# Splitting the loads of keys and values by partitions over two DMA queues

## The chip, the cores and the metric

The kernel runs on one core of one Trainium2 chip. The metric is device time in microseconds (us) from the start to the end of one execution; lower is better. The core has engines with instruction streams of their own: TensorE (PE; weight loads are listed as PEld), VectorE (DVE), ScalarE (ACT), GpSimd (POOL) and SyncE (SP). They meet only through semaphores. DMA engines, sixteen of them in the profile, carry data between the chip's memory (HBM) and the on-chip memory (SBUF), which has 128 partitions (rows). A DMA is issued by an engine into that engine's queue.

## What is computed

One decoding step of grouped-query attention over a long cache, in parallel with a small MLP, both added to the input:

```python
Hq, Hkv, Sk, Dh = 32, 8, 65536, 128          # D = 512, Dff = 1792, one token
xn = layernorm(x)
q = (xn @ wq).reshape(1, 1, Hq, Dh)          # 4 query heads share one key head
scores = einsum("bhqd,bhkd->bhqk", q, k) * Dh ** -0.5
o = einsum("bhqk,bhkd->bhqd", softmax(scores), v)
out = x + o.reshape(1, 1, Hq * Dh) @ wo + maximum(xn @ w1, 0) @ w2
```

All is float32. Keys and values are 8 heads x 65536 x 128 x 4 bytes each, 537 MB together, out of the 561 MB that the profile shows as read.

## The kernel before

The attention goes over 8 key heads (`HKV`) with 4 steps (`NP`) each, 32 steps (`STEPS`). A step handles 16384 keys. Its keys are one load of 128 rows (the head dimension) x 16384 float32 into the buffer `ks`; its values are one load of 128 rows x 16384 float32 into `vs`. In both, a row is 65,536 bytes without a break. There is one `ks` and one `vs`, no second buffer of either.

The order of the work is written out by hand, with one instruction stream per engine and semaphores between them:

- **SyncE** issues all of the loads. The first keys are issued near the beginning (line 175), behind the loads of `wq`. Then, head by head, `head(h)` calls `v_load` and `k_load` in turn, so its queue holds keys 0, values 0, keys 1, values 1 and so on. `k_load` (lines 303 to 305) waits for `k_free`, `v_load` (lines 307 to 310) for `v_free`. A `Fori` loop runs seven heads, with the next head's first keys at the end of each; the eighth head follows it. After that SyncE issues `w1` and `w2` into `ks`, and, when `vs` is free, `wo` into `vs`.
- **TensorE** runs a loop of 32 steps. It waits for the keys (`k_in`, line 346), makes the scores from `ks` into PSUM (line 352), takes part in a maximum over partitions (lines 357 to 359), waits for the values (`v_in`, line 363) and for the weights of the softmax (`s_w`), and makes the products with `vs` (line 368).
- **VectorE** transposes the scores (line 384), finds the running maximum, and adds the products into `acc` (lines 408 and 410). Its wait for the last scores frees the keys (`k_free`), its wait for the products frees the values (`v_free`). At the end of a head it reduces (lines 416 to 423).
- **ScalarE** runs 8 x 4 times: wait for `s_bias` (line 428), four exponentials with their sums (line 430), from the second step on one for the rescaling (line 436). At the end of each head it waits for `s_diff` (line 440) and runs one more exponential (line 441).

The lines that matter most:

```python
def k_load(h, n):
    sy.wait_ge(k_free, 1).then_inc(k_free, -1)
    sy.dma_start(ks, k[h, 0, :, n * NT * KEYS : (n + 1) * NT * KEYS]).then_inc(k_in, 16)
...
te.wait_ge(k_in, 16).then_inc(k_in, -16)
...
te.wait_ge(v_in, 16).then_inc(v_in, -16)
```

A DMA adds 16 to its semaphore when it has landed, so 16 means one whole load.

Of the kernel before, what the change touches and what calls it, by code (L numbers as in the profile page):

```python
# [10 lines left out]
ALU = mybir.AluOpType  # L11
AX = mybir.AxisListType
PSUM = bass.MemoryType.PSUM
ENG = mybir.EngineType

P = 128
D = 512
HQ, HKV, DH = 32, 8, 128
# [5 lines left out]
SUB = TW // 32  # L24
KEYS = CT * TW
# [3 lines left out]
NT = 8  # L29
NP = TPC // NT  # L30
# [39 lines left out]
def attention_and_mlp_kernel(  # L70
# [28 lines left out]
    nc = tc.nc  # L99
    scale = float(DH) ** -0.5  # L100
    te, ve, se, ge, sy = nc.tensor, nc.vector, nc.scalar, nc.gpsimd, nc.sync

    def place(name, *shape, rows=P):
        return nc.alloc_sbuf_tensor(name, [rows, *shape], F32).ap()

    def bank(name, *shape):
        return nc.alloc_psum_tensor(name, [P, *shape], F32).ap()

    ks = place("ks", NT * KEYS)
    vs = place("vs", NT * KEYS)  # L110
# [32 lines left out]
    pa, pb = bank("pa", 2, TW), bank("pb", 2, TW)  # L143
    acc_o, acc_z, acc_y, pm = (bank(n, 512) for n in ("acc_o", "acc_z", "acc_y", "pm"))

    names = "k_in v_in tiles scores m_out bias_out a_out w_out o_out k_free v_free q_in d_out f_out f_free"
    (
        k_in, v_in, s_tiles, s_dve, s_max, s_bias, s_alpha, s_w, s_o,
        k_free, v_free, q_in, s_diff, f_out, f_free,
    ) = (nc.alloc_semaphore(n) for n in names.split())  # L150
    PE, DV, AC, GP = (Flow(nc, e, n) for e, n in ((te, "pe"), (ve, "dve"), (se, "act"), (ge, "pool")))

# [32 lines left out]
    def memset(flow, ap, value):  # L185
        return flow.op(lambda e: e.memset(ap, value))

    d = memset(DV, ones, 1.0)
    d = memset(DV, x4, 0.0)
    x4_free = DV.mark  # L190
    d = memset(DV, qcur, 0.0)
# [108 lines left out]
    AC.need(DV.mark)  # L300


    def k_load(h, n):
        sy.wait_ge(k_free, 1).then_inc(k_free, -1)
        sy.dma_start(ks, k[h, 0, :, n * NT * KEYS : (n + 1) * NT * KEYS]).then_inc(k_in, 16)

    def v_load(h, n):
        sy.wait_ge(v_free, 1).then_inc(v_free, -1)
        src = v[h].rearrange("(p t b) d -> p t (b d)", p=P, b=SUB)
        sy.dma_start(vs, src[:, n * NT : (n + 1) * NT, :].rearrange("p t f -> p (t f)")).then_inc(v_in, 16)  # L310

    def head(h):
        v_load(h, 0)
        for n in range(1, NP):
            k_load(h, n)
            v_load(h, n)

    sy.wait_ge(*wq_read)
    sy.sem_inc(v_free, 1)
    with nc.Fori(0, HKV - 1, engines=[ENG.SP]) as h:  # L320
        head(h)
        k_load(h + 1, 0)
# [20 lines left out]


    with nc.Fori(0, STEPS, engines=[ENG.PE]):
        te.wait_ge(k_in, 16).then_inc(k_in, -16)
        te.wait_ge(q_in, 1).then_inc(q_in, -1)  # L347
        for s in range(NT):
            tile_of = (pa, pb)[s // 2 % 2][:, s % 2, :]
            for c in range(CT):  # L350
                at = (s * CT + c) * TW
                i = te.matmul(tile_of[32 * c : 32 * c + 32, :], qcur, ks[:, at : at + TW], start=True, stop=True)  # L352
                if c == 0 and s in (4, 6):
                    i._wait_ge(s_dve, s // 2 - 1)
            if s % 2:
                i.then_inc(s_tiles, 1)
        te.transpose(pm[:G, :P], m, ident)._wait_ge(s_dve, 3).then_inc(s_max, 1)  # L357
        te.matmul(pm[:, P : P + G], ones[:G, :], dg[:, :G], start=True, stop=True)._wait_ge(s_dve, 4)  # L358
        te.matmul(  # L359
            pm[:, P + G : P + G + 1], rowg, dg[:, G : G + 1], start=True, stop=True  # L360
        ).then_inc(s_max, 1)
        te.sem_inc(s_dve, -4)
        te.wait_ge(v_in, 16).then_inc(v_in, -16)
        te.wait_ge(s_w, 1).then_inc(s_w, -1)  # L364
        n = NT * SUB // WIDE
        for i in range(n):
            c = i % CT
            mm = te.matmul(  # L368
                acc_o[32 * c : 32 * c + WIDE * G, :],
                wt[:, i * WIDE : (i + 1) * WIDE, :].rearrange("p b g -> p (b g)"),  # L370
                vs[:, i * 512 : (i + 1) * 512],
                start=(i < CT), stop=(i >= n - CT),
            )
        mm.then_inc(s_o, 1)
# [48 lines left out]
        ve.reduce_sum(fin[:, :DH], masked.rearrange("p b d -> p d b"), axis=AX.X).then_inc(f_out, 1)  # L423


    with nc.Fori(0, HKV, engines=[ENG.Activation]):
        for n in range(NP):
            se.wait_ge(s_bias, 1).then_inc(s_bias, -1)  # L428
            for g in range(G):
                i = se.activation(  # L430
                    wt[:, :, g], tr[:, :, g], AF.Exp, bias=bias[:, n, g : g + 1],
                    scale=scale, accum_out=part[:, n, g : g + 1],
                )
            i.then_inc(s_w, 1)
            if n:
                se.activation(
                    alpha[:, n : n + 1], bias[:, n - 1, G : G + 1], AF.Exp,
                    bias=bias[:, n, G : G + 1], scale=-1.0,
                ).then_inc(s_alpha, 1)
        se.wait_ge(s_diff, 1).then_inc(s_diff, -1)  # L440
        se.activation(
            fac.rearrange("p n g -> p (n g)"), diff.rearrange("p n g -> p (n g)"), AF.Exp
        ).then_inc(s_alpha, 1)
# [157 lines left out]
```

## Time and profile before

| what | us |
|---|---|
| median of 3 runs | 1303.62 |
| lowest and highest of them | 1303.43, 1303.95 |
| the profiled execution | 1303.08 |
| its span in the profile | 1301.8 |

The profile is of one execution, traced by the hardware. Its span runs from the first to the last instruction; the time of that execution is 1.3 us longer. Line numbers (L352) are those of the kernel before. "PEq", "ACTq" and "SPq" are the engines' sequencers, which wait and issue; "out<-in" names the tensors that an instruction writes and reads. In a row of the timeline the first two numbers are start and duration in us; in square brackets stands how long the engine had been idle, and what released it.

### The profile page before, as it was taken

The numbers are of one execution on the slowest core, as the hardware profiler recorded it, in microseconds if no ns is written. First come the engines' busy times: TensorE is split into PE (matmuls) and PEld (weight loads), VectorE is DVE, ScalarE is ACT, GpSimd is POOL, SyncE is SP. The second block draws the span as 40 slices with busy tenths as digits, with TensorE's granted clock in tenths as the row PEclk, the third lists the DMA queues.
The fourth block names the chain that finished last, engine by engine and source line by source line (L and its number), as shares of the span: only waits on it lengthen the run. The fifth ranks groups of instructions, "written<-read, shape, count | busy, mean of one in ns | idle before, by whom it ended". The sixth has DMA issues, their size and how long they took to land. (4 is left out here: it accounts for less than half of the span.)

```text
span 1301.8 us, 10655 instructions
## 1 busy us (share of the span) xinstructions
PE 657.1 (50%) x4512; PEld 184.1 (14%) x4512; DVE 268.5 (21%) x398; ACT 76.0 (6%) x292; POOL 4.1 (0%) x22
## 2 busy tenths in 40 slices
PE   3455455445445445535535544534544644544558
PEld 1111111111111111111111111111111111111112
DVE  2221122222112222112222112222112222201222
ACT  0000000000000000000000000000000000000000
POOL 0000000000000000000000000000000000000000
PEclk9677777677677677677677768777767767666769
DMA  9999999999999999999999999999999999999998
GB/s 419 419 449 421 449 421 449 419 437 433 431 439 421 449 421 449 421 449 419 437 433 427 443 421 449 421 449 421 449 419 437 433 423 447 421 449 421 449 417 360
DMA packets 11101, 561.06 MB, mean 431 GB/s; under 512 B 1492, under 2 KB 1496, under 8 KB 1880
## 3 DMA queue, kind: packets, MB, share of 16 engines
q1 hardware_dynamic: 10944, 561.00, 99.7%
q8 instruction: 3, 0.05, 0.0%
q10 hardware_dynamic: 152, 0.00, 0.0%
q14 instruction: 2, 0.02, 0.0%
HBM read 560.99 MB, written 0.00 MB: 431 GB/s over the span
## 5 line engine op out<-in xcount | busy, mean ns | idle before, releaser
L368 PE MATMUL acc_o<-vs,wt 128*16 128x512 f32 x2048 | 291.0, 732 | 183.7 <-PEq L364 183.7
L352 PE MATMUL pa<-ks,qcur 128*32 128x512 f32 x1024 | 174.8, 815 | 327.3 <-PEq L347 327.3
L384 DVE STREAM_TRANSPOSE tr<-pa 128x1024 f32<-128x1024 f32 x64 | 80.0, 1250 | 414.6 <-PE pa L352 414.6
L352 PE MATMUL pb<-ks,qcur 128*32 128x512 f32 x1024 | 137.6, 656 | 0.0
L430 ACT ACTIVATE wt<-tr,bias 128x128 f32<-128x128 f32 x128 | 64.3, 511 | 1082.4 <-ACTq L428 1082.4
L368 PEld LDWEIGHTS acc_o<-vs,wt 128*16 128x16 f32 x2048 | 69.2, 112 | 378.8 <-issue 378.8
L352 PEld LDWEIGHTS pa<-ks,qcur 128*32 128x32 f32 x1024 | 39.0, 134 | 434.2 <-issue 425.4
L410 DVE SCALAR_TENSOR_TENSOR acc<-acc,alpha,acc_o 128x512 f32<-128x512 f32 x24 | 17.9, 748 | 354.2 <-PE acc_o L368 354.2
L384 DVE STREAM_TRANSPOSE tr<-pb 128x1024 f32<-128x1024 f32 x64 | 80.0, 1250 | 47.8 <-PE pb L352 47.8
L352 PEld LDWEIGHTS pb<-ks,qcur 128*32 128x32 f32 x1024 | 41.2, 129 | 105.5 <-issue 86.3
L357 PE MATMUL pm<-ident,m 128*4 128x128 f32 x32 | 10.0, 313 | 87.7 <-DVE m L396 67.2
L408 DVE COPY acc<-acc_o 128x512 f32<-128x512 f32 x8 | 5.5, 692 | 119.7 <-PE acc_o L368 119.7
L358 PE MATMUL pm<-dg,ones 4*128 4x4 f32 x64 | 15.0, 302 | 21.4 <-DVE dg L400 21.4
L393 DVE TENSOR_REDUCE mc<-tr 128x4 f32<-128x512 f32 x24 | 24.1, 1006 | 1.8
L430 ACT ACTIVATION_READ_ACCUMULATOR wt<-tr,bias 128x1 f32 x128 | 23.9, 187 | 0.0
L357 PEld LDWEIGHTS pm<-ident,m 128*4 128x4 f32 x32 | 2.6, 81 | 116.8 <-DVE m L396 89.0
L358 PEld LDWEIGHTS pm<-dg,ones 4*128 4x128 f32 x64 | 12.2, 236 | 28.8 <-DVE dg L400 28.8
L288 PE MATMUL pa<-vs,tr 128*8 128x512 f32 x64 | 10.3, 803 | 8.3 <-DMA vs<-wq 7.0
L359 PE MATMUL pm<-dg,rowg 4*128 4x1 f32 x64 | 14.3, 290 | 0.0
L359 PEld LDWEIGHTS pm<-dg,rowg 4*128 4x128 f32 x64 | 13.0, 249 | 0.0
L398 DVE TENSOR_REDUCE mg<-pm 4x1 f32<-4x128 f32 x32 | 8.9, 279 | 13.0 <-PE pm L357 13.0
L401 DVE COPY bias<-pm 128x5 f32<-128x5 f32 x32 | 5.2, 164 | 27.9 <-PE pm L359 27.9
(98 smaller groups left out, 104.6 us busy)
## 6 DMA issues: line engine op xcount, KB each, us to landing
vs<-wq SPq DMA_DIRECT2D x1, 7168.0 KB, 21.4
ks<-w SPq DMA_DIRECT2D x2, 3584.0 KB, 21.7
vs<-wo SPq DMA_DIRECT2D x3, 2048.0 KB, 17.4
vs<-wq SPq DMA_DIRECT2D x1, 1024.0 KB, 4.9
vs<-wo SPq DMA_DIRECT2D x1, 1024.0 KB, 23.9
ks<-k SPq DMA_DIRECT2D x32, 29.1
vs<-v SPq DMA_DIRECT2D x32, 29.1
vs<-wo SPq DMA_DIRECT2D x1, 512.0 KB, 24.7
```

What stands on the lines that cost most here:

```text
L288: lambda e: e.matmul(pr[32 * c : 32 * c + HKV, :], xs[:, i, :], vs[:, i * 512 : (i + 1) * 512], start=(i < CT), stop=(i >= SLICES - CT),),
L352: i = te.matmul(tile_of[32 * c : 32 * c + 32, :], qcur, ks[:, at : at + TW], start=True, stop=True)
L357: te.transpose(pm[:G, :P], m, ident)._wait_ge(s_dve, 3).then_inc(s_max, 1)
L358: te.matmul(pm[:, P : P + G], ones[:G, :], dg[:, :G], start=True, stop=True)._wait_ge(s_dve, 4)
L359: te.matmul(pm[:, P + G : P + G + 1], rowg, dg[:, G : G + 1], start=True, stop=True).then_inc(s_max, 1)
L368: mm = te.matmul(acc_o[32 * c : 32 * c + WIDE * G, :], wt[:, i * WIDE : (i + 1) * WIDE, :].rearrange("p b g -> p (b g)"), vs[:, i * 512 : ...
L384: i = ve.transpose(tr[:, s * SUB : (s + 2) * SUB, :].rearrange("p b i -> p (b i)"), (pa, pb)[s // 2 % 2].rearrange("p i k -> p (i k)"),)._ ...
L393: i = ve.reduce_max(top, tr[:, :, :G].rearrange("p b g -> p g b"), axis=AX.X)
L398: ve.reduce_max(mg, pm[:G, :P], axis=AX.X)._wait_ge(s_max, 1)
L408: ve.tensor_copy(flat, acc_o)
L410: ve.scalar_tensor_tensor(flat, flat, alpha[:, n : n + 1], acc_o, op0=ALU.mult, op1=ALU.add)
L430: i = se.activation(wt[:, :, g], tr[:, :, g], AF.Exp, bias=bias[:, n, g : g + 1], scale=scale, accum_out=part[:, n, g : g + 1],)
```

## The change

Each load after the first keys is issued as two DMAs of 64 partitions. SyncE still waits for the free buffer; it then issues rows 0 to 63 and raises a new semaphore (`k_pass` or `v_pass`). ScalarE waits for that and issues rows 64 to 127 on its own queue. On ScalarE the two issues stand at the head of each step, before its wait for `s_bias`: first the lower half of this step's values, then the lower half of the next step's keys. For the last step of a head these keys belong to the next head, and a counter in a register with a branch leaves them out after the last head. TensorE waits for 32 instead of 16. The first keys stay one DMA; SyncE adds the missing 16 itself.

```diff
+    upper, lower = slice(0, P // 2), slice(P // 2, P)
+
+    def k_half(e, half, h, n):
+        e.dma_start(ks[half], k[h, 0, half, n * NT * KEYS : (n + 1) * NT * KEYS]).then_inc(k_in, 16)
+
+    def v_half(e, half, h, n):
+        src = v[h].rearrange("(p t b) d -> p t (b d)", p=P, b=SUB)
+        e.dma_start(
+            vs[half], src[half, n * NT : (n + 1) * NT, :].rearrange("p t f -> p (t f)")
+        ).then_inc(v_in, 16)
+
     def k_load(h, n):
         sy.wait_ge(k_free, 1).then_inc(k_free, -1)
-        sy.dma_start(ks, k[h, 0, :, n * NT * KEYS : (n + 1) * NT * KEYS]).then_inc(k_in, 16)
+        k_half(sy, upper, h, n)
+        sy.sem_inc(k_pass, 1)
 
     def v_load(h, n):
         sy.wait_ge(v_free, 1).then_inc(v_free, -1)
-        src = v[h].rearrange("(p t b) d -> p t (b d)", p=P, b=SUB)
-        sy.dma_start(vs, src[:, n * NT : (n + 1) * NT, :].rearrange("p t f -> p (t f)")).then_inc(v_in, 16)
+        v_half(sy, upper, h, n)
+        sy.sem_inc(v_pass, 1)
+
+    def k_rest(h, n):
+        se.wait_ge(k_pass, 1).then_inc(k_pass, -1)
+        k_half(se, lower, h, n)
+
+    def v_rest(h, n):
+        se.wait_ge(v_pass, 1).then_inc(v_pass, -1)
+        v_half(se, lower, h, n)
...
     sy.wait_ge(*wq_read)
     sy.sem_inc(v_free, 1)
+    sy.sem_inc(k_in, 16)
...
-        te.wait_ge(k_in, 16).then_inc(k_in, -16)
+        te.wait_ge(k_in, 32).then_inc(k_in, -32)
...
-        te.wait_ge(v_in, 16).then_inc(v_in, -16)
+        te.wait_ge(v_in, 32).then_inc(v_in, -32)
...
-    with nc.Fori(0, HKV, engines=[ENG.Activation]):
+    heads_left = nc.alloc_registers("heads_left", engines=[ENG.Activation])
+    nc.regs_mov(heads_left, HKV)
+    with nc.Fori(0, HKV, engines=[ENG.Activation]) as h:
         for n in range(NP):
+            v_rest(h, n)
+            if n < NP - 1:
+                k_rest(h, n + 1)
+            else:
+                nc.regs_alu(heads_left, heads_left, 1, op=ALU.subtract)
+                se.br_lt(heads_left, 1, on_true="last_keys", on_false="next_keys")
+                with nc.body("next_keys", valid_engines=[ENG.Activation]):
+                    k_rest(nc.s_assert_within(h + 1, 0, HKV - 1, skip_runtime_bounds_check_because="the branch"), 0)
+                    nc.br("last_keys", engines=[ENG.Activation])
+                nc.switch_bb("last_keys")
             se.wait_ge(s_bias, 1).then_inc(s_bias, -1)
```

More of the change, by code (lines that the diff above doesn't have):

```diff
@@ L144, in attention_and_mlp_kernel @@
     acc_o, acc_z, acc_y, pm = (bank(n, 512) for n in ("acc_o", "acc_z", "acc_y", "pm"))
-    names = "k_in v_in tiles scores m_out bias_out a_out w_out o_out k_free v_free q_in d_out f_out f_free"
+    names = "k_in v_in tiles scores m_out bias_out a_out w_out o_out k_free v_free q_in d_out f_out f_free k_pass v_pass"
     (
         k_in, v_in, s_tiles, s_dve, s_max, s_bias, s_alpha, s_w, s_o,
-        k_free, v_free, q_in, s_diff, f_out, f_free,
+        k_free, v_free, q_in, s_diff, f_out, f_free, k_pass, v_pass,
     ) = (nc.alloc_semaphore(n) for n in names.split())
```

## The prediction

> **What bounds the kernel now.** I read the page's first lines, then the busy times by windows, the waits, the timeline of the first two steps, and the chain of waits at the end.
>
> ```profile
> span 1301.8 us, 10655 instructions
> PE 657.1 (50%) x4512; PEld 184.1 (14%) x4512; DVE 268.5 (21%) x398; ACT 76.0 (6%) x292; POOL 4.1 (0%) x22
> DMA  9999999999999999999999999999999999999998
> q1 hardware_dynamic: 10944, 561.00, 99.7%
> ```
>
> No engine is busy for more than half of the span; the DMA engines are busy in every slice, nearly all of it on one queue (q1, SyncE's). The next view is the row of busy times for one long window, from the first keys' landing to the last keys' landing; its last three columns are the TensorE clock, the mean busy share of the 16 DMA engines, and GB/s. Beneath it stands line 347, the wait for keys, with the times of its first and last passing.
>
> ```profile
> 42.20:1243.20 1201.00, 598.50 (x4123) 168.29 (x4123) 246.90 (x337) 70.55 (x278) 2.92 (x14) 0.73 1.00 433
> L347 PEldq EVENT_SEMAPHORE  x32: 51/51/51, 42.2 to 1243.2; - x32
> ```
>
> From the first to the 32nd landing of keys lie 31 loads of keys and 31 of values: 1201.0 / 62 = **19.37 us a load**. A load is 128 rows of 16384 float32, 65,536 B a row, 8.389 MB; 8.389 MB / 19.37 us = 433 GB/s, as the row says. The share is 1.00, so at most 0.5% of 1201 us, 6 us, is idle. The kernel is a stream of loads without a gap, and its time is bytes over rate.
>
> Does compute ever hold a load back? Here is the timeline of the first two steps:
>
> ```profile
> 31.66 0.35 SPq L310 DMA_DIRECT2D vs<-v  x1
> 42.27 3.64 PE L352 MATMUL pa<-ks,qcur 128*32 128x512 f32 x16 [9.62 <-PEq L347]
> 52.32 0.34 SPq L305 DMA_DIRECT2D ks<-k  x1
> 56.96 0.52 ACT L430 ACTIVATE wt<-tr,bias 128x128 f32<-128x128 f32 x1 [46.90 <-ACTq L428]
> 58.86 0.19 ACT L430 ACTIVATION_READ_ACCUMULATOR wt<-tr,bias 128x1 f32 x1
> 62.86 9.67 PE L368 MATMUL acc_o<-vs,wt 128*16 128x512 f32 x64 [6.23 <-PEq L364]
> 72.78 0.33 SPq L310 DMA_DIRECT2D vs<-v  x1
> 82.21 3.40 PE L352 MATMUL pa<-ks,qcur 128*32 128x512 f32 x16 [9.68 <-PEq L347]
> ...
> 95.43 0.52 ACT L430 ACTIVATE wt<-tr,bias 128x128 f32<-128x128 f32 x1 [36.38 <-ACTq L428]
> ```
>
> Keys land at 42.27, the scores have read them by 52.32 and the next keys are issued, 10.5 us before the values ahead of them in the queue land (62.86). Values land at 62.86, are used up by 72.78, and the next values are issued 9.4 us before the keys ahead land (82.21). Each load therefore waits in the queue about 10 us, and compute is hidden. The end is the same stream:
>
> ```profile
> 1272.90 23.92 DMA vs<-wo
> 1296.86 1.16 PE acc_z L513 x8
> 1298.05 0.70 DVE rows L544
> ```
>
> The last weights land, and about 5 us of work follows. Only the rate of the loads, or a gap between them, can move the time by more than a few us.
>
> **The change, part by part.** *Bytes:* the same. *Issues:* each of 63 loads (32 of values, 31 of keys; the first keys at line 175 stay whole) becomes two DMAs of 64 rows, one on SyncE's queue, one on ScalarE's.
>
> ```profile
> L305 SPq DMA_DIRECT2D ks<-k x31: 328/333/338, 52.3 to 1213.6; - x31
> 0.76 0.41 ACTq L157 DMA_DIRECT2D xT<-x  x1
> 3.32 1.08 ACTq L157 DMA_DIRECT2D x<-x  x1
> ACT wt L430 <- ACTq L428: 1082.4, 32, 46.9
> ```
>
> SyncE's issue still costs 0.33 us. ScalarE gains 63 issues of 0.41 to 1.08 us, 26 to 68 us in all, beside 1082 us in which it waits before line 430. I cost them at nothing; the cover is place by place. The lower keys go out after SyncE passes them on at 52.3 + 0.33, plus at most 1.1, so by 53.8, and the exponentials start at 56.96: 3.2 us of cover. The lower values go out at about 73.5 to 74.2; the next exponentials start at 95.43, 21 us later.
>
> *New waits:* ScalarE waits on v_pass, then k_pass, ahead of each step's s_bias. Behind them stand this step's exponentials, and behind those TensorE's products with the values. In the old order of time both passes come first (step 0: 31.66 and 52.32 against 56.96; step 1's values: 72.78 against 95.43), so nothing is held. Once a head the lower values also stand behind line 441:
>
> ```profile
> 188.79 0.75 DVE L410 SCALAR_TENSOR_TENSOR acc<-acc,alpha,acc_o 128x512 f32<-128x512 f32 x1 [15.54 <-PE acc_o L368]
> 188.93 0.34 SPq L310 DMA_DIRECT2D vs<-v  x1
> 189.90 0.21 ACT L441 ACTIVATE fac<-diff 128x12 f32<-128x12 f32 x1 [14.25 <-ACTq L440]
> ```
>
> SyncE issues its half at 188.93, ScalarE is free at 190.1, so that half is about 1.2 us late, under the 9.4 us that a load waits in its queue anyway: nothing. TensorE's waits for 32 instead of 16 cost nothing by themselves; they end with the later half. The branch and register steps on ScalarE run 8 times in idle time.
>
> *The start:* V0's lower half (V0, K1 and so on count the loads in order) no longer stands behind the whole load of K0 but runs beside it. At the old rate K0, with 42.3 - 32.7 = 9.6 us left, shares with half a load of 9.7 us and lands near 51.9. Its scores take 52.32 - 42.27 = 10.05 us, so K1 is issued near 61.9, and V0's upper half ends at 62.8 as before, the bytes being the same. The exponentials end 58.86 + 0.19 - 42.27 = 16.8 us after the keys' landing, at 68.7, the products take 9.9, and V1 is issued at 78.6, still 3.6 us before K1 lands near 82.2. How soon a DMA starts is in these two windows:
>
> ```profile
> 0.00:2.00 2.00, 0.00 (x0) 0.00 (x0) 0.00 (x0) 0.00 (x0) 0.20 (x4) 1.00 0.21 33
> 2.00:4.00 2.00, 0.00 (x0) 0.00 (x0) 0.86 (x5) 0.00 (x0) 0.50 (x2) 1.00 0.84 324
> ```
>
> Of the first 4 us, 0.42 + 1.68 are busy; 1.9 are lost, 0.75 of them before the first issue. So a start costs about 1.15 us, of which 0.9 are covered here: 0 to 1.2 us once, and I take 0.3.
>
> *The rate of a load of 64 rows:* the term that decides. No row shows one, for every large load writes all 128 rows. It has two bounds. If 433 GB/s belongs to the sixteen engines, wherever they write, two halves take 2 x 9.69 = 19.37 us, and nothing changes. If it belongs to the rows written, 433 / 128 = 3.4 GB/s a row, half the rows give 217 GB/s, and a half alone takes 19.37 us. Two halves in two queues would then still reach 433 only while half of the engines write upper rows and the others lower ones. Nothing arranges this: SyncE always issues first and ScalarE follows within about 1.5 us, so every engine finds the upper half first and the lower one second, and all of them change sides together. An engine that ran ahead would run dry, and start its next load with the upper half beside the others again. So by that bound a load costs 2 x 19.37 = 38.74 us, 19.37 more.
>
> I take the second bound. Sum: 63 x 19.37 = 1220 us; with 0 for the issues and waits (at 38.7 us a load, the other load covers compute with 28 us more to spare, and the start gap is gone as well); the tail behind the last values is of 128-row loads and stays. Profiled execution 1303.08 (span 1301.8 and 1.3 around it) + 1220 = **2523 us**; the median shown, 1303.62, is 0.5 us off that execution, which changes nothing here.
>
> [...]
>
> **Rivals.** *B, engines own the rate (not slower).* The mechanism: sixteen engines each move one row at a time, and two queues only change the order. For it: the share of 1.00 at a steady 433 GB/s is what engines at their own limit show. Against it: a limit of the rows would show the same, and no large load in the trace has another row count. Time 1303.1 + 0 to 1.2, so **1303.4**; it decides if a row written beside 63 others moves as fast as beside 127. If in this case the two queues drift apart by a whole half load, the next load's remainder at a landing is 9.7 us against 10.05 of scores plus 1.15 of start: 1.5 us of gap, and at 62 loads up to 93 us, 1396.
>
> *C, rows own it but the engines get out of step.* A pair that shares rows and changes sides at different moments loses only while both are on one side. For it: the two queues are issued at different moments, and K0 whole beside V0's lower half starts engines unequally. Against: the restarts above. Half the loss gives 1303 + 610 = **1913**.
>
> *D, a gain.* A second queue fills the seams between loads. The share of 1.00 leaves at most 6 us: **1297 to 1301**.
>
> **How the numbers follow.** Between the two bounds of the rate the trace decides nothing, so I start even, and take 0.15 off for C and 0.03 for D: 0.41 each. I move 0.14 towards the slow bound, since full rate needs 64 rows to take what only 128 have been seen to take, and since the change offers nothing on the other side: no gap to fill. A 0.55, B 0.27 (0.20 with no difference, 0.07 with a drift), C 0.15, D 0.03. The measurement can tell about 0.2%, 2.6 us, from no change. So slower 0.55 + 0.15 + 0.07 = 0.77, same 0.20, faster 0.03. A and B hold 0.82 and lie at the two ends, so the range has to span them: 1301 to 2550, the upper end being the sum plus 1% for late halves. A's own range goes from half way to C, 2218, to 2550.
>
> **What would show it.** In A the page's GB/s falls to about 217 with the DMA share still near 1.00, both queues carry about half the bytes, the waits for keys at line 347 end 77.5 us apart, two loads of 38.7, and TensorE's idle time before lines 352 and 368 grows by about 1200 us. In B GB/s stays at 433 and the first keys are used near 52 instead of 42.27. In C GB/s lies between, and the landings are uneven. ScalarE's exponentials later than 4.6 us after the keys are free would show that its issues do cost. I am wrong if a half load alone, or two side by side, moves at 433 GB/s.

## The result, and the profile after

| what | us |
|---|---|
| before, median (lowest to highest) | 1303.53 (1303.21 to 1303.95) |
| changed, median of 4 runs (lowest to highest) | 2559.88 (2517.18 to 2583.84) |
| changed, the profiled execution (its span) | 2545.54 (2544.1) |
| ratio to the kernel before | 1.9423, 95% interval 1.9354 to 1.9492 |

The ratio leaves out the two longest runs of the changed kernel, which count as disturbed, and so corresponds to 1303.53 x 1.9423 = 2532 us, under the median of all four. The changed kernel takes nearly twice as long. The first lines of its page:

```profile
span 2544.1 us, 10974 instructions
PE 660.3 (26%) x4512; PEld 184.3 (7%) x4512; DVE 268.5 (11%) x398; ACT 76.0 (3%) x292; POOL 4.1 (0%) x22
...
DMA  9999999999999999999999999999999999999999
GB/s 347 214 214 214 214 214 214 214 214 214 214 214 214 214 214 214 217 216 214 216 221 215 215 214 214 214 215 214 214 214 214 214 214 214 214 214 214 214 214 314
...
q1 hardware_dynamic: 6912, 296.75, 51.5%
q10 hardware_dynamic: 5192, 264.25, 48.4%
...
L389 PE MATMUL acc_o<-vs,wt 128*16 128x512 f32 x2048 | 293.5, 737 | 802.0 <-PEq L385 802.0
L373 PE MATMUL pa<-ks,qcur 128*32 128x512 f32 x1024 | 175.8, 819 | 946.4 <-PEq L368 946.4
```

Every engine is as busy as before in microseconds (TensorE 660.3 against 657.1), and the bytes are the same, now about half on each queue. The DMA engines are busy in every slice, and yet move 214 to 221 GB/s wherever the loads are split; only the first and the last slices (347 and 314), with their loads of 128 rows, are faster. So the share of 9 in the DMA line is no sign of a full rate: here the busy DMA engines carry half as much, 214 GB/s against the 433 of before. What grew is TensorE's idle time before the scores (line 373, from 327.3 to 946.4 us) and before the products (line 389, from 183.7 to 802.0), 619.1 + 618.3 = 1237 us together, close to the 1242.3 by which the span grew. The rows of before, with the idle time in us, how often, and the longest:

```profile
PE pa L352 <- PEq L347: 327.3, 32, 11.0
PE acc_o L368 <- PEq L364: 183.7, 32, 6.8
```

The waits for keys (line 367 now) and for values (line 384), and the busy times between the first and the last wait for keys:

```profile
L367 PEldq EVENT_SEMAPHORE  x32: 51/51/51, 53.0 to 2473.8; - x32
L384 PEldq EVENT_SEMAPHORE  x32: 51/51/51, 93.0 to 2503.8; - x32
```

```profile
53.00:2473.80 2420.80, 603.60 (x4123) 169.25 (x4123) 246.84 (x337) 70.54 (x278) 2.92 (x14) 0.61 1.00 215
```

2420.8 / 62 = 39.05 us a load, against 19.37: 2.02 times. The rows above name the wait that stands right behind the one for the load (L347 and L368 for the query, L364 and L385 for the softmax weights) and is passed 0.1 to 0.2 us after it; what is waited for is the load. The timeline of the first step shows that the issues are not what is late:

```profile
31.94 0.58 SPq L310 DMA_DIRECT2D vs<-v  x1
33.69 0.55 ACTq L310 DMA_DIRECT2D vs<-v  x1
53.27 3.64 PE L373 MATMUL pa<-ks,qcur 128*32 128x512 f32 x16 [20.42 <-PEq L368]
...
63.17 0.47 SPq L306 DMA_DIRECT2D ks<-k  x1
63.92 0.48 ACTq L306 DMA_DIRECT2D ks<-k  x1
...
67.78 0.52 ACT L463 ACTIVATE wt<-tr,bias 128x128 f32<-128x128 f32 x1 [57.63 <-ACTq L461]
```

ScalarE's half follows SyncE's by 0.75 us for the keys and by 1.75 for these first values, and its exponentials start 67.78 - 53.27 = 14.5 us after the keys, no later than the 56.96 - 42.27 = 14.7 of before.

### The profile page after: what moved, and what is told of

It is laid out like the page before. It is cut to its first block, busy times and chain, and to the rows that moved or that the text cites. A ratio compares the mean times of both kernels' runs of the same rounds, so it can differ in the third digit from the quotient of the medians.

```text
span 2544.1 us, 10974 instructions
## 1 busy us (share of the span) xinstructions
PE 660.3 (26%) x4512; PEld 184.3 (7%) x4512; DVE 268.5 (11%) x398; ACT 76.0 (3%) x292; POOL 4.1 (0%) x22
## 5 line engine op out<-in xcount | busy, mean ns | idle before, releaser
L389 PE MATMUL acc_o<-vs,wt 128*16 128x512 f32 x2048 | 293.5, 737 | 802.0 <-PEq L385 802.0
L373 PE MATMUL pa<-ks,qcur 128*32 128x512 f32 x1024 | 175.8, 819 | 946.4 <-PEq L368 946.4
L546 PE MATMUL acc_z<-vs,sw 128*1 128x512 f32 x56 | 10.1, 592 | 2.1 <-DMA vs<-wo 2.1
```

The lines of the kernel that those rows point to most:

```text
L389: mm = te.matmul(acc_o[32 * c : 32 * c + WIDE * G, :], wt[:, i * WIDE : (i + 1) * WIDE, :].rearrange("p b g -> p (b g)"), vs[:, i * 512 : ...
L546: lambda e: e.matmul(acc_z[32 * c : 32 * c + 1, :], lhsT, row, start=c not in begun, stop=last),
```

## The experiments

All kernels differ from the changed one only as shown. What is compared is the time and the GB/s in a long window of the steady stretch (the columns are those of the windows above; the last two are the busy share of the DMA engines and GB/s). In the same stretch the kernel before and the changed kernel have these rows:

```profile
100.00:1240.00 1140.00, 568.28 (x3921) 159.40 (x3921) 232.71 (x319) 66.19 (x261) 2.92 (x14) 0.73 1.00 433
```

```profile
100.00:2440.00 2340.00, 581.02 (x3982) 162.94 (x3978) 239.43 (x328) 68.45 (x270) 2.92 (x14) 0.61 1.00 215
```

The theory is that the rows written in the on-chip memory set the rate; the rivals are two queues taking turns, the number of rows or of DMAs, and the addresses read in HBM.

**Halves by columns on two queues.** Each DMA takes all 128 rows and half of the columns.

```diff
-        e.dma_start(ks[half], k[h, 0, half, n * NT * KEYS : (n + 1) * NT * KEYS]).then_inc(k_in, 16)
+        w = NT * KEYS // 2
+        at = half * w
+        e.dma_start(ks[:, at : at + w], k[h, 0, :, n * NT * KEYS + at : n * NT * KEYS + at + w]).then_inc(k_in, 16)
```

(and the same for the values).

> The same two queues and the same two DMAs a load as in the changed kernel, but each DMA takes all 128 rows and half of the columns (32,768 B a row). If the rows written set the rate, a load is back at 19.37 us: 1303 us, within 3 us. If taking turns between two queues is what costs, the rows make no difference and the time stays near 2540 us.

Measured: 1308.59 us, ratio 1.0041 (1.0027 to 1.0056).

```profile
100.00:1240.00 1140.00, 576.03 (x3921) 161.35 (x3921) 231.84 (x318) 67.03 (x266) 2.92 (x14) 0.72 1.00 432
```

Two queues, two DMAs a load, ScalarE's issues and the new waits are all still there, and the loss is gone but for 5.6 us, which was not expected and is taken up below. Queues and waits are not the cause.

**Halves by rows on one queue.** The mirror image: the split stays, the second queue goes.

```diff
-        k_half(sy, upper, h, n)
-        sy.sem_inc(k_pass, 1)
+        k_half(sy, upper, h, n)
+        k_half(sy, lower, h, n)
```

(the values alike; ScalarE's issues and waits are removed).

> The two halves by rows, 0 to 63 and 64 to 127, both issued by SyncE on one queue, upper first; ScalarE issues nothing. If the rows written set the rate, each half takes 19.4 to 19.5 us by itself and the time is 2500 to 2580 us, as with two queues. If the two queues are the cause, the time goes back to about 1303 us.

Measured: 2636.52 us, ratio 2.0230 (2.0189 to 2.0270), 57 us over the range that was expected.

```profile
100.00:2500.00 2400.00, 574.85 (x3926) 161.27 (x3926) 238.72 (x327) 68.46 (x270) 2.94 (x14) 0.61 1.00 207
```

The split by rows alone brings the whole loss. The second queue even helps by a little, 215 GB/s against 207.

**Even and odd rows on two queues.**

```diff
-    upper, lower = slice(0, P // 2), slice(P // 2, P)
+    upper, lower = slice(0, P, 2), slice(1, P, 2)
```

> The halves are the even and the odd rows instead of the upper and the lower ones; queues and number of rows as in the changed kernel. If 64 rows of one side, 0 to 63 or 64 to 127, share half of the ways in, each half now reaches both sides and the time goes back to about 1303 us. If it is the number of rows that sets the rate (3.4 GB/s a row), 64 rows stay at 217 GB/s and the time at about 2540 us. A time between would say that engines meet on a finer pattern of rows.

Measured: 1304.06 us, ratio 1.0009 (0.9999 to 1.0020).

```profile
100.00:1240.00 1140.00, 574.74 (x3921) 161.46 (x3921) 232.60 (x319) 66.15 (x261) 2.92 (x14) 0.72 1.00 434
```

One line, the same 64 rows a DMA, and all of the loss is gone. So it is not the number of rows. It is which rows.

**Quarters, by neighbours and by every fourth row.** First, each half as two DMAs of 32 neighbouring rows.

```diff
     def k_half(e, half, h, n):
-        e.dma_start(ks[half], k[h, 0, half, n * NT * KEYS : (n + 1) * NT * KEYS]).then_inc(k_in, 16)
+        for r in (slice(half.start, half.start + 32), slice(half.start + 32, half.stop)):
+            e.dma_start(ks[r], k[h, 0, r, n * NT * KEYS : (n + 1) * NT * KEYS]).then_inc(k_in, 16)
```

(the values alike, and TensorE waits for 64).

> Each half is issued as two DMAs of 32 rows on its queue. If the rate goes by the number of rows, 32 rows take 108 GB/s, a load takes 77.5 us, and the time is 1303 + 63 x 58.1 = about 4960 us. If it goes by the side (0 to 63 or 64 to 127), 32 rows are as fast as 64 and the time stays near 2540 us.

Measured: 2598.65 us, a single run.

```profile
100.00:2500.00 2400.00, 598.79 (x4050) 168.82 (x4042) 240.13 (x329) 68.46 (x270) 2.94 (x14) 0.61 1.00 211
```

32 neighbours are nearly as fast as 64, 211 against 215 GB/s. Then the same four DMAs a load, with every fourth row each:

```diff
-    upper, lower = slice(0, P // 2), slice(P // 2, P)
+    upper, lower = (slice(0, P, 4), slice(1, P, 4)), (slice(2, P, 4), slice(3, P, 4))
```

> Four DMAs of 32 rows a load, two per queue, as with the quarters, but each takes every fourth row of the 128 instead of 32 neighbours. If it is the span of the rows that decides, about 1304 to 1310 us, a row 2.42 us. If small numbers of rows or many DMAs cost anything by themselves, it goes towards the 2599 us of the quarters.

Measured: 1303.71 us, ratio 1.0028 (0.9994 to 1.0061), no difference from before that can be told. Two of the eight runs took 1313.8 and 1316.4 us, the others 1303.2 to 1303.8; why is not known.

```profile
100.00:1240.00 1140.00, 567.41 (x3921) 158.57 (x3921) 232.76 (x319) 66.55 (x264) 2.94 (x14) 0.73 1.00 433
```

32 rows a DMA, four DMAs a load, two queues: the full rate of before, 433 GB/s. Neither few rows nor many DMAs cost anything here.

**Sixteen neighbours.** The same edit as for the quarters with slices of 16 rows, eight DMAs a load.

> Eight DMAs of 16 neighbouring rows a load, four per queue. [...] If every row of a load with fewer than 128 neighbours just takes twice as long, whatever the span, a row stays at 4.9 us and the time near 2600 us.

Measured: 4628.54 us, ratio 3.5516 (3.5099 to 3.5934).

```profile
200.00:4400.00 4200.00, 530.61 (x3926) 149.21 (x3926) 238.81 (x327) 68.46 (x270) 2.94 (x14) 0.57 1.00 117
```

The rate drops once more, to 117 GB/s, little over a quarter of 433, with the DMA engines' share at 1.00 as ever. A row takes 8.97 us, not 4.9, so among blocks under 128 rows the rate is not the same whatever their size. Rates by the neighbours in one DMA: 128 rows 433, 64 rows 215, 32 rows 211, 16 rows 117 GB/s.

**Source and destination apart.** In one kernel the rows 0 to 63 of the source go to even places and the rest to odd ones; in the other the even rows of the source go to places 0 to 63. `strided` maps the half's start to every second row.

```diff
-        e.dma_start(ks[half], k[h, 0, half, n * NT * KEYS : (n + 1) * NT * KEYS]).then_inc(k_in, 16)
+        e.dma_start(ks[strided[half.start]], k[h, 0, half, n * NT * KEYS : (n + 1) * NT * KEYS]).then_inc(k_in, 16)
```

> Source and destination taken apart, first part: the rows 0 to 63 of the source go to the even rows of the buffers, rows 64 to 127 to the odd rows; queues as in the changed kernel. The rows of keys and values thereby stand in other places than the products assume, all else is computed as before. If the rows written in SBUF set the rate, about 1304 us as with even and odd rows throughout. If the rows read in HBM set it (each 262,144 B from the next), about 2540 us as in the changed kernel.

```diff
-        e.dma_start(ks[half], k[h, 0, half, n * NT * KEYS : (n + 1) * NT * KEYS]).then_inc(k_in, 16)
+        e.dma_start(ks[half], k[h, 0, strided[half.start], n * NT * KEYS : (n + 1) * NT * KEYS]).then_inc(k_in, 16)
```

> Source and destination taken apart, second part: the even rows of the source go to rows 0 to 63 of the buffers, the odd rows to 64 to 127; the rows again stand in other places than the products assume. If the rows written set the rate, about 2540 us; if the rows read set it, about 1304 us.

Measured, a single run each: 1306.83 us with even places, 2579.27 us with even sources. The window of the first, then of the second:

```profile
100.00:1240.00 1140.00, 577.84 (x3924) 162.23 (x3923) 232.84 (x320) 68.43 (x270) 2.94 (x14) 0.72 1.00 433
```

```profile
100.00:2500.00 2400.00, 585.07 (x4018) 164.15 (x4010) 240.16 (x329) 68.45 (x270) 2.92 (x14) 0.61 1.00 212
```

The time follows the places written (433 GB/s into even and odd places, 212 into blocks); the order of the rows read makes no such difference.

**Sixty-four rows by themselves.** Only SyncE's half is issued; ScalarE's issues are removed, and TensorE waits for 16.

> Only the upper half of each load after the first keys is issued, by SyncE, on one queue; rows 64 to 127 keep what stood there, so half of the keys and values is left out. A measurement of 64 rows by themselves. If they take 217 GB/s, half the bytes take the old time: 1303 us, up to 1340 with the 207 GB/s that one queue showed. If 64 rows alone take 433 GB/s, a load takes 9.7 us, compute becomes the limit with about 27 us a step, and the time is near 930 us.

Measured: 1371.61 us, a single run.

```profile
100.00:1200.00 1100.00, 515.41 (x3587) 144.49 (x3587) 216.12 (x295) 61.44 (x244) 2.93 (x14) 0.72 1.00 205
```

Half of the bytes take longer than all of them did before. One half by itself moves at 205 GB/s with no second queue and no other half near it, so neither is needed for the loss. The time is over the 1340 us that were expected at most. In part that bound was added up too low: at 207 GB/s the 4.194 MB of a half take 20.26 us, so 63 of them give 1303 + 63 x 0.89 = 1359. The rest is the rate: at 205 GB/s a half takes 20.46, which gives 1303 + 63 x 1.09 = 1372.

**The small costs.** Even and odd rows, both on SyncE's queue (the edit of even and odd rows in the kernel of one queue):

> Even and odd rows as two DMAs a load, both on SyncE's queue. If the 1 us over the kernel before of even and odd rows on two queues is what V0's early half costs at the start, this is back at 1303.0 us within 0.5. If it comes from the number of DMAs, it stays at 1304 us.

Measured: 1303.99 us, ratio 1.0007 (0.9997 to 1.0016). It did not go back to 1303.0, but against the 1303.3 of the runs beside it this is within what can be told from no change, as the 1304.06 on two queues is. What V0's early half costs stays unsettled below 1 us.

Halves by columns, both on SyncE's queue:

> Halves by columns, all 128 rows, both on SyncE's queue. The same halves on two queues took 1308.6 us, 5.6 more than before. If the shorter rows (32,768 B) cost that, the time stays near 1308 us; if it is the two queues, it goes back to 1303 us.

Measured: 1309.21 us, ratio 1.0046 (1.0029 to 1.0062). With one queue the columns cost 6.1 us over the 1303.12 of the runs beside it, so the 5.6 us are not the queues' but the shorter rows'. In the DMA records of the trace a row of 65,536 B takes 2.422 us on average in the kernel before, and two of 32,768 B take 2 x 1.217 = 2.434; as an estimate, at 128 / 16 = 8 rows an engine and 63 loads that is about 6 us.

**Engines out of step.** The prediction said that two halves side by side lose because all engines write into the same half at the same time. One DMA of eight rows, once, was to push some of the engines a row behind the others.

```diff
     sy.wait_ge(*wq_read)
+    aside = nc.dram_tensor("aside", (8, NT * KEYS), F32, kind="Internal").ap()
+    set_aside = load(sy, "set_aside", aside, k[0, 0, :8, : NT * KEYS])
```

> The changed kernel with one DMA more, once, ahead of the first values on SyncE's queue: eight rows of 65,536 B from HBM to a place in HBM that nobody reads. If it runs on eight of the sixteen engines, those fall about one row behind the others. If the halves lose because all engines write into the same side at the same time, and the engines that meet are one of the eight and one of the others, this one shift moves the time far below 2540 us, towards 1303. If the engines come back into step, or those that meet are shifted alike, it stays within the spread of the changed kernel, 2517 to 2584 us. If a side has half of the rate whoever writes into it and both sides can't work at once, it stays there as well.

Measured: 2587.62 us, ratio 1.9856 (1.9817 to 1.9896).

```profile
100.00:2500.00 2400.00, 592.47 (x4054) 166.64 (x4054) 240.15 (x329) 68.47 (x270) 2.93 (x14) 0.61 1.00 212
```

No gain: the time lies just above the changed kernel's spread, 2517 to 2584. The counts that follow are from the DMA records between 100 us and the last 60 us; SyncE's queue writes rows 0 to 63, ScalarE's rows 64 to 127, and sixteen rows are under way at a time. In the changed kernel all sixteen were in one half for 69% of the time, so its engines are in step. Here it is 3%, but both halves had at least four rows at once for only 35% of the time (12% in the changed kernel), so the step was loosened rather than broken.

The few rows that were written out of step tell more. A row with on average eight or fewer others beside it on its own half still took about 4.9 us. For 61 rows no more than one other row was in their half at any moment, and for four of these none at all; they took 5.08 us on average, about as long as the rows of the upper halves alone (5.11), where all sixteen are in one half. So it is not the half that is shared by whoever writes into it: a row of a block of neighbours is slow even with its half to itself or nearly so, while the others are written into the other half. What holds it there was not settled; the records do not name the engine that moved a row. The mean durations of a row of 65,536 B in the records, in the same stretch:

| kernel | us a row |
|---|---|
| before; even and odd; every fourth row | 2.42 |
| changed | 4.88 |
| quarters of neighbours | 4.98 |
| halves by rows, one queue | 5.07 |
| upper halves alone | 5.11 |
| sixteen neighbours | 8.97 |

No kernel here beats the one before. It moves its bytes at 433 GB/s, and no split that was tried moved them measurably faster.

## Why the prediction was right, step by step

**The bound before: right.** Only the rate of the loads could move the time by more than a few us, and it did. Compute stayed hidden: the engines' busy times are unchanged (TensorE 657.1 and 660.3 us, VectorE 268.5 in both), and the growth of TensorE's idle time is waiting for loads, 1237 us of the 1242 by which the span grew. One reading was off without effect: line 347 is not the wait for keys but the one right behind it. The keys' own, line 346, is passed 42.0 to 1243.0, both 0.2 us earlier, so the 19.37 stands.

**Issues, new waits, branch at nothing: right.** The columns on two queues keep all of them and cost 5.6 us, and those come from the rows' length. ScalarE's issues took 0.48 and 0.55 us, inside the 0.41 to 1.08 given; SyncE's rose from 0.33 to 0.47, which is hidden as well.

**The start: right in size.** K0 was to land near 51.9; the scores start at 53.27.

**A load of 64 rows, the term that decides: the bound taken held, 19.37 us more a load.** It measured 39.05 - 19.37 = 19.68. The miss against the profiled execution, 2545.5 - 2523.4 = 22 us, is mostly this: 62 x 0.31 = 19 us. The rest lies at the ends. By the waits for keys and values themselves (before: lines 346 and 363, the latter passed last at 1262.4) the first keys land 11.0 us later, the last values 30.0 us after the last keys instead of 19.4, and 0.9 is added behind: 22.5 in all, against 19.37 for the 63rd load, 3 us. The median of all four runs, 2559.88, is above the upper end that was given, 2550; the 2532 that the ratio gives is inside.

**The reason given for it: half right.** The prediction put 3.4 GB/s on each row written. That the rows written set the rate is shown by source and destination taken apart (433 and 212 GB/s). That it goes by their number is not so: 32 neighbours move nearly as fast as 64 (211 against 215 GB/s), and 64 or 32 rows spread over the 128 move at 434 and 433 GB/s. It goes by how the rows lie: blocks of 64 and 32 neighbours move at about half of 433 GB/s, blocks of 16 at 117. What makes a block slow no run here shows; that rows of one side "share half of the ways in" was the author's guess.

**In step: it happens, but it is not the reason.** "All of them change sides together" was why two halves side by side could not share the rate. They do change together, with all sixteen rows in one half for 69% of the time. But the prediction's half rate is shared by those who write into a half, so a row alone in its half should be fast, and the rows that were nearly alone took 5.08 us; with the step loosened the rate stayed at 212 GB/s. The price came out right because a block of neighbours is slow by itself (205 GB/s). That two halves side by side do not make up for it is shown; by what mechanism is open. In this part the right number was luck.

**The rivals.** B, engines own the rate, is refuted by 205 GB/s of upper halves alone. C, partial overlap, did not occur even for the rows that were out of step (5.08 us a row). D, a gain at the seams, did not occur: the spread splits stay at 1303.7 to 1304.1 us, against 1303.0 to 1303.3 for the kernel before in the runs beside them.

## What to carry to other kernels

A load that fills 128 partitions with long rows, as here, should stay one DMA over all of them, or be split by columns or by every second or fourth row: 433 GB/s whole, 432 by columns, 434 and 433 by every second and fourth row. A split into blocks of 64 or 32 neighbouring rows halved the rate (215 and 211 GB/s), and blocks of 16 left about a quarter (117). When a load is slow, read GB/s beside the busy share: the DMA engines were fully busy at 433, at 215 and at 117 GB/s. And before splitting a load over queues, ask whether there is a gap to fill: a share of 1.00 at a steady rate left at most 6 us to win here.

## What the runs showed of the hardware that was not expected

Blocks of 64 rows go a little faster from two queues than from one: 215 against 207 GB/s, a row 4.88 against 5.07 us, though the two halves never gain the full rate. Rows half as long cost 0.5% with all 128 partitions, 2.434 against 2.422 us for the same bytes. A row of a block of 64 neighbours takes about 5 us even when nearly all of the others under way go into the other half: 61 rows with at most one other in their half took 5.08. And the changed kernel's four runs spread over 67 us, 2517 to 2584, where the kernel before stays within 1 us; no run was made to find out why.
